# Attention by pairs of heads in whole float32 for all batches, ahead of a feed-forward network, on one core

## The chip, the cores and the metric

The kernel runs on one core of a Trainium2 chip. A core has a matrix engine (TensorE, PE in the profile, with its weight loads as PEld), VectorE (DVE), ScalarE (ACT), GpSimd (POOL) and a queue engine (SyncE, SP), each with an instruction stream of its own. The metric is the device time of one launch in microseconds.

## The reference

Sliding-window attention with a linear bias per head, and behind it a two-layer network with a sigmoid-weighted activation. Cut to what is computed:

```
# q, k, v: [8, 8, 576, 64]; w_in: [512, 2048]; w_out: [2048, 512]; all float32
scores = q @ k.transpose(0, 1, 3, 2) / sqrt(64)
rel    = pos[:, None] - pos[None, :]
slopes = 2.0 ** (-8.0 * (arange(8) + 1) / 8)
scores = where((rel >= 0) & (rel < 128), scores - slopes * abs(rel), -1e9)
attn   = softmax(scores)                      # + 1e-9 in the denominator
x      = (attn @ v).transpose(0, 2, 1, 3).reshape(4608, 512)
h      = x @ w_in
out    = (h * sigmoid(1.702 * h)) @ w_out     # [4608, 512] float32
```

## The kernel before

The 4608 rows of the network are cut into 18 chunks of 256 (`T`). A `Job` is one chunk against the 16 blocks of 128 hidden units (`DFF`); `up` makes one hidden block (twelve matmuls of 256 columns, L569) and `down` adds it to the output (six of 512 columns, L588). The network works in the reduced format F32R: each operand is split into a high part and a remainder, and three of the four products are kept. The weights come as 64-bit words and are decoded on the chip (L228 to L235), two halves per hidden block, just ahead of their first use.

Attention makes the chunks' inputs. It is cut into units, and every call of `tick` moves several units one stage on: loads, scores, bias and minimum (`biased`), exponentials (`exponents`), division (`normal`), transposes (`flip`), products with the values (`mix`). `due` lists by which chunk how many units must be through, and from which chunk on they may start; the main loop calls `tick` between hidden blocks at the pace that this asks. Within that the order on each engine is made by a scheduler with a simulated timeline; `in_turn` fixes the order of a group of matmuls, and `tc.keep_in_program_order` pins an instruction to its place in the program.

There are two kinds of units:

- Batches 1 to 7 use `Unit`. A pair of heads stands end to end as 1152 positions in nine blocks of 128, cut into five units of one or two blocks. q and k are laid out twice, on rows 0 to 63 and 64 to 127. Q holds the high part of q on the upper half and its remainder on the lower; K1 and K2 hold high part and remainder of k on both. A score block is two full-array products, Q with K1 and Q with K2 (L351). The values stand as high part beside remainder (`VV`), the transposed probabilities are split into `ph` and `pl` (L475, L481), and each block of keys takes two products (L516). Rows 0 to 63 and 64 to 127 of the result are added by `sum_up` (L537 to L546).
- Batch 0 uses `WholeUnit`: a third of the sequence (0 to 256, 256 to 512, 512 to 576) for two heads together, one on rows 0 to 63 and the other on rows 64 to 127 of the array. Scores are float32 products with a contraction of 64 (L341). The two heads' products with the values go to the two column halves (L496). Nothing is split or added up. The second head's scores use a tile of the transposes' pair of PSUM tiles (`t_ps`).

PSUM's eight banks are `acc0`, `acc1`, two `h_ps`, `s_ps`, two `t_ps` and `x_ps`. The first four units run before the network starts ("early"), with idle matmuls on the identity between them (`spin`), and the first weights are decoded in that stretch (`DECODE_TICKS`).

Of the kernel before, what the change touches and what calls it, by code (L numbers as in the profile page):

```python
# [20 lines left out]
P = 128  # L21
# [14 lines left out]
BESIDE = range(12, 24)  # L36
DECODE_TICKS = 4, 5, 6, 7
FETCH_AHEAD = 6
DECODE_AHEAD = 2
# [6 lines left out]
class Block:  # L46


    def __init__(self, q0, rows, heads, first=0, live=0):
        self.q0, self.rows = q0, rows  # L50
        self.heads = heads
        self.first = first
        self.live = live
        self.end = P + rows


class Chunk:


    def __init__(self, pos, n, parts):  # L60
        self.pos, self.n, self.parts = pos, n, parts
        self.width = sum(b.rows for b, _ in parts)
        self.x0 = parts[0][0].q0


class Segment:


    def __init__(self, pos, cols, carried, chunks):
        self.pos, self.cols, self.carried = pos, cols, carried  # L70
        self.first, self.last = chunks[0], chunks[-1]
        for c in chunks:
            c.segment = self


class Unit:


    whole = False

    def __init__(self, pair, blocks, loaded, chunks):
        self.pair, self.blocks = pair, blocks
        self.loaded = loaded
        self.chunks = chunks


def pair_blocks(hp):

    A, Z = 2 * hp, 2 * hp + 1
    blocks = []  # L90
    for i in range(L // P):
        first = P if i == 0 else 0
        live = HALF if i == 5 else first
        if i == 4:
            heads = [(A, 0, HALF, 0), (Z, HALF, P, P + HALF)]
        else:
            heads = [(A if i < 4 else Z, 0, P, live)]
        blocks.append(Block(i * P, P, heads, first, live))
    return blocks


def whole_batch(b):
    units = []
    for hp in range(NP):
        blocks = pair_blocks(hp)
        n = len(blocks)
        chunks = [Chunk(i * P, P, [(blocks[i], P)] + [(z, 0) for z in blocks[i + 1:i + 2]]) for i in range(n)]
        for i in range(0, n, 3):
            Segment(i * P, 3 * P, P if i + 3 < n else 0, chunks[i:i + 3])
        done = 0  # L110
        for i in range(0, n, 2):
            upto = min(i + 1, n) if i + 2 < n else n
            units.append(Unit(b * NP + hp, blocks[i:i + 2], chunks[i:i + 2], chunks[done:upto]))
            done = upto
    return units


def some_blocks(b, runs):

    units = []  # L120
    for hp in range(NP):
        for first, end in runs:
            blocks = pair_blocks(hp)[first:end]
            chunks = [Chunk((first - 1) * P, P, [(blocks[0], 0)])] if first else []
            lead = len(chunks)
            for i, bk in enumerate(blocks):
                chunks.append(Chunk(bk.q0, P, [(bk, P)] + [(z, 0) for z in blocks[i + 1:i + 2]]))
            Segment(first * P, (end - first) * P, 0, chunks)
            pair = b * NP + hp
            if len(blocks) > 2:  # L130
                units.append(Unit(pair, blocks[:2], chunks[:lead + 2], chunks[:lead + 1]))
                units.append(Unit(pair, blocks[2:], chunks[lead + 2:], chunks[lead + 1:]))
            else:
                units.append(Unit(pair, blocks, chunks, chunks))
    return units


class WholeUnit:

    whole = True

    def __init__(self, hp, lo, hi):
        self.hp, self.lo, self.hi = hp, lo, hi
# [9 lines left out]
def part_batch(lo, hi):  # L155
    return [WholeUnit(hp, lo, hi) for hp in range(NP)]
# [3 lines left out]
def tile_kernel(ctx: ExitStack, tc: tile.TileContext, q0, k0, v0, qT, kT, v, w_in, w_out, out):  # L160
# [59 lines left out]
    def decode(st, name):  # L220
# [7 lines left out]
        nc.scalar.activation(c.bitcast(F32), top.bitcast(F32), AF.Copy, scale=2.0 ** -112)  # L228
        nc.vector.tensor_scalar(low, low, 29, None, ALU.logical_shift_right)
        nc.vector.scalar_tensor_tensor(c, c, 3, low, ALU.logical_shift_left, ALU.bitwise_or)  # L230
        nc.vector.scalar_tensor_tensor(c, top, -0x80000000, c, ALU.bitwise_and, ALU.bitwise_or)
        w = c.bitcast(F32)
        res = const.tile([P, 2, 512], F32R, name=name, tag=name)
        nc.scalar.copy(res[:, 0], w)
        nc.gpsimd.tensor_tensor(res[:, 1], w, res[:, 0].bitcast(F32), ALU.subtract)  # L235
        return res
# [4 lines left out]
    def spread(pair, pos, n):  # L241

        b = pair // NP
        at = 0
        while at < n:
            hh, s = divmod(pos + at, S)
            c, o = divmod(b * S + s, T)
            m = min(n - at, S - s, T - o)
            yield hh, c, o, at, m
            at += m  # L250

    def load(u):
        if u.whole:
            load_whole(u)
            return
        b0, bz = u.blocks[0], u.blocks[-1]
        u.q0, u.nq = b0.q0, bz.q0 + bz.rows - b0.q0
        u.k0 = b0.q0 - P + b0.first
        u.nk = u.q0 + u.nq - u.k0
        u.rq = raw.tile([P, 2 * P], F32, name="rq", tag="rq")  # L260
        u.rk = raw.tile([P, 3 * P], F32, name="rk", tag="rk")
        move(u.rq[:, :u.nq], qT[u.pair - NP, :, u.q0:u.q0 + u.nq])
        move(u.rk[:, :u.nk], kT[u.pair - NP, :, u.k0:u.k0 + u.nk])

    def load_whole(u):
# [9 lines left out]
        move(u.rq[:, :u.hi - u.lo], q0[u.hp, :, u.lo:u.hi])  # L275
        if u.early:
            tc.keep_in_program_order(nc.scalar.dma_start(u.rk[:, :u.hi - u.k0], k0[u.hp, :, u.k0:u.hi]))
        else:
            move(u.rk[:, :u.hi - u.k0], k0[u.hp, :, u.k0:u.hi])
        if not u.early:  # L280
            load_whole_v(u)

    def load_whole_v(u):
        full = (u.hi - u.k0) // P
        end = u.k0 + full * P
        move(u.rv[:, :full], v0[u.hp, u.k0:end].rearrange("(c p) h d -> p c h d", p=P))
        if end < u.hi:
            move(u.rv[:u.hi - end, full], v0[u.hp, end:u.hi])

    def load_v(u):  # L290
        if u.whole:
            return
        u.rv = raw.tile([P, 3, D], F32, name="rv", bufs=2)
        at = u.loaded[0].pos
        full = sum(c.n == P for c in u.loaded)
        u.spans = []
        if full:
            move(u.rv[:, :full], v[u.pair - NP, at:at + full * P, :].rearrange("(c p) d -> p c d", p=P))
            u.spans.append((P, slice(0, full)))
        if full < len(u.loaded):  # L300
            m = u.loaded[-1].n
            move(u.rv[:m, full], v[u.pair - NP, at + full * P:at + full * P + m, :])
            u.spans.append((m, slice(full, full + 1)))

    def split_q(u):
        if u.whole:
            return
        u.Q = att.tile([P, 2 * P], F32R, name="Q")
        nc.scalar.copy(u.Q[:, :u.nq], u.rq[:, :u.nq])  # L309

    def split_v(u):
        if u.whole:
            return
        u.VV = att.tile([P, 3, 2, D], F32R, name="VV", bufs=3)
        for m, cs in u.spans:
            nc.scalar.copy(u.VV[:m, cs, 0, :], u.rv[:m, cs])
            nc.gpsimd.tensor_tensor(u.VV[:m, cs, 1, :], u.rv[:m, cs], u.VV[:m, cs, 0, :].bitcast(F32), ALU.subtract)
        for i, c in enumerate(u.loaded):
            c.v = u.VV[:c.n, i].rearrange("p a d -> p (a d)")

    def split_rest(u):
        if u.whole:
            return
        u.K1 = att.tile([P, 3 * P], F32R, name="K1")
        u.K2 = att.tile([P, 3 * P], F32R, name="K2")
# [145 lines left out]
    def high(u):  # L471
        if u.whole:
            return
# [323 lines left out]
```

## Time and profile before

| | |
|---|---|
| median of 3 runs | 1090.27 us (1087.84 to 1092.25) |
| profiled execution | 1090.57 us, its span 1088.8 us |
| busy: PE, DVE, POOL, ACT | 1050.6, 730.2, 644.7, 603.0 us |
| mean granted clock of TensorE | 0.984 |
| instructions | 21667 |
| DMA | 81.24 MB, mean 75 GB/s |

Times are in us unless marked ns. A row of the groups reads: line, engine, operation, output from inputs by the program's names, shapes, count, then busy time and mean ns of one, then idle time of the engine just before them and what ended it. Matmuls are pipelined and their ends are modelled; what one costs in a row of them is seen from the distance of starts. A float32 matmul shows as more than one record.

### The profile page before, as it was taken

The numbers are of one execution on the slowest core, as the hardware profiler recorded it, in microseconds if no ns is written. First come the engines' busy times: TensorE is split into PE (matmuls) and PEld (weight loads), VectorE is DVE, ScalarE is ACT, GpSimd is POOL, SyncE is SP. The second block draws the span as 40 slices with busy tenths as digits, with TensorE's granted clock in tenths as the row PEclk, the third lists the DMA queues.
The fourth block names the chain that finished last, engine by engine and source line by source line (L and its number), as shares of the span: only waits on it lengthen the run. The fifth ranks groups of instructions, "written<-read, shape, count | busy, mean of one in ns | idle before, by whom it ended". The sixth has DMA issues, their size and how long they took to land.

```text
span 1088.8 us, 21667 instructions
## 1 busy us (share of the span) xinstructions
PE 1050.6 (96%) x7013; PEld 939.0 (86%) x7013; DVE 730.2 (67%) x2260; ACT 603.0 (55%) x1812; POOL 644.7 (59%) x919
## 2 busy tenths in 40 slices
PE   6897889999999999999999999999999999999998
PEld 3576777998898999999999999999999999998997
DVE  6979788678888787754666768676867677413131
ACT  5674696466665666543555566655565556322222
POOL 3788897566676676644565556666666666323232
PEclk8896999999999999999999999999999999999999
DMA  6357322232322222211122212222222212000000
GB/s 205 123 178 286 99 70 71 81 84 70 98 75 82 69 84 68 79 28 48 54 70 59 74 54 84 66 84 56 84 67 67 68 53 64 1 20 21 1 20 20
DMA packets 93298, 81.24 MB, mean 75 GB/s; under 512 B 42752, under 2 KB 84480, under 8 KB 93184
## 3 DMA queue, kind: packets, MB, share of 16 engines
q1 hardware_dynamic: 87424, 69.89, 22.3%
q10 hardware_dynamic: 5760, 9.96, 2.5%
q8 instruction: 55, 0.90, 0.4%
q14 instruction: 59, 0.48, 0.1%
HBM read 70.39 MB, written 9.44 MB: 73 GB/s over the span
## 4 chain that ended last, share of the span: by engine, by line
PE 81%; DVE 3%; ACT 0%; issue 0%; DVEq 0%
PE h_ps L569 34%; PE acc L588 33%; PE x_ps L516 5%; PE s_ps L351 5%; PE t_ps L462 4%; DVE xh L553 0%; DVE K L327 0%; DVE xl L555 0%; DVE pb L379 0%; DVE pb L426 0%; DVE pl L481 0%; DVE xf L546 0%; DVE g L575 0%; ACT pb L398 0%; DVE rec L409 0%
## 5 line engine op out<-in xcount | busy, mean ns | idle before, releaser
L569 PE MATMUL h_ps<-xh,w 128*128 128x256 f32 x2304 | 371.4, 286 | 7.5 <-DVE g L575 5.2
L579 POOL TENSOR_TENSOR gl<-g,gh 128x256 fp32r<-128x256 f32 x288 | 217.8, 757 | 260.0 <-ACT gh L578 196.7
L569 PEld LDWEIGHTS h_ps<-xh,w 128*128 128x128 f32 x2304 | 330.4, 190 | 36.4 <-DVE g L575 7.4
L588 PE MATMUL acc<-w,gh 128*128 128x512 f32 x1152 | 326.5, 401 | 0.2 <-DVE o L604 0.2
L575 DVE SCALAR_TENSOR_TENSOR g<-g,h_ps 128x256 f32<-128x256 f32 x288 | 119.2, 415 | 184.7 <-ACT g L574 183.0
L574 ACT ACTIVATE g<-h_ps 128x256 f32<-128x256 f32 x288 | 109.8, 382 | 218.4 <-PE h_ps L569 188.5
L588 PEld LDWEIGHTS acc<-w,gh 128*128 128x128 f32 x1152 | 197.4, 189 | 27.4 <-issue 0.4
L569 PE MATMUL h_ps<-xl,w 128*128 128x256 f32 x1152 | 198.8, 282 | 1.8 <-DVE xl L555 0.9
L588 PE MATMUL acc<-w,gl 128*128 128x512 f32 x576 | 187.7, 401 | 0.4 <-POOL gl L579 0.3
L578 ACT CAST gh<-g 128x256 fp32r<-128x256 f32 x288 | 116.4, 405 | 124.8 <-DVE g L575 113.9
L329 POOL TENSOR_TENSOR K<-rk,K 128x384 fp32r<-128x384 f32 (+1 forms) x140 | 130.1, 929 | 76.7 <-ACT Q L309 13.5
L569 PEld LDWEIGHTS h_ps<-xl,w 128*128 128x128 f32 x1152 | 166.0, 189 | 8.8 <-POOL xl L555 1.2
L398 ACT ACTIVATE pb<-pb,mins 128x256 f32<-128x256 f32 (+2 forms) x252 | 122.4, 487 | 56.7 <-DVE mins L379 51.8
L328 POOL TENSOR_TENSOR Q<-rq,Q 64x256 fp32r<-64x256 f32 (+1 forms) x140 | 99.4, 710 | 25.9 <-DVE K L327 3.4
L379 DVE CUSTOM_DVE_ANT_0 pb<-s_ps,bias 128x128 f32<-128x128 f32 (+2 forms) x280 | 100.2, 376 | 9.7 <-PE s_ps L351 5.8
L588 PEld LDWEIGHTS acc<-w,gl 128*128 128x128 f32 x576 | 92.3, 188 | 8.9 <-POOL gl L579 0.8
L426 DVE TENSOR_SCALAR pb<-pb,rec 128x256 f32<-128x256 f32 (+2 forms) x229 | 97.4, 462 | 3.3
L351 PE MATMUL s_ps<-K,Q 128*128 128x256 f32 (+1 forms) x504 | 92.0, 288 | 4.7 <-DVE mins L379 3.2
L481 DVE TENSOR_TENSOR pl<-t_ps,ph 128x512 fp32r<-128x512 f32 (+2 forms) x140 | 84.1, 603 | 12.1 <-ACT ph L475 7.2
L409 DVE TENSOR_SCALAR rec<-sums 128x2 f32<-128x2 f32 (+3 forms) x152 | 51.4, 338 | 56.6 <-ACT pb L398 52.7
L462 PE MATMUL t_ps<-ident,pb 128*128 128x128 f32 x476 | 86.5, 273 | 1.0 <-DVE pl L481 1.0
L351 PEld LDWEIGHTS s_ps<-K,Q 128*128 128x128 f32 x504 | 74.5, 189 | 12.3 <-DVE mins L379 2.8
(70 smaller groups left out, 1328.3 us busy)
## 6 DMA issues: line engine op xcount, KB each, us to landing
rk<-kT SPq DMA_DIRECT2D x84, 192.0 KB, 2.5
rq<-qT SPq DMA_DIRECT2D x112, 128.0 KB, 2.4
out<-o ACTq DMA_DIRECT2D x36, 256.0 KB, 2.5
rw<-w_in SPq DMA_DIRECT2D x16, 512.0 KB, 4.3
rw<-w_out SPq DMA_DIRECT2D x16, 512.0 KB, 5.5
rk<-kT SPq DMA_DIRECT2D x56, 128.0 KB, 2.2
rv<-v SPq DMA_DIRECT2D x100, 64.0 KB, 2.0
rq<-qT SPq DMA_DIRECT2D x28, 64.0 KB, 2.3
```

Source lines behind the costliest of these rows:

```text
L328: nc.gpsimd.tensor_tensor(Q[D:], rq[D:], Q[D:].bitcast(F32), ALU.subtract)
L329: nc.gpsimd.tensor_tensor(K2, rk, K1.bitcast(F32), ALU.subtract)
L351: nc.tensor.matmul(u.s[:b.rows, e, b.first:b.end], u.Q[:, b.q0 - u.q0:b.q0 - u.q0 + b.rows], k[:, ko:ko + b.end - b.first], start=(z == 0) ...
L379: nc.vector.tensor_tensor_reduce(b.p[ra:rb, cs:b.end], u.s[ra:rb, e, cs:b.end], bias[head][ra:rb, cs:b.end], -SCALE, BIG, ALU.add, ALU.min ...
L398: nc.scalar.activation(live, live, AF.Exp, bias=u.mins[:b.rows, e:e + 1], scale=-1.0, accum_out=u.sums[:b.rows, e:e + 1],)
L462: nc.tensor.transpose(u.t[:c.n, w:w + b.rows], b.p[:b.rows, col:col + c.n], ident[:b.rows, :b.rows])
L569: nc.tensor.matmul(h, w1[f][:, z, k * P:(k + 1) * P], x[:, k], start=(n == 0), stop=(n == len(ops) - 1))
L574: nc.scalar.activation(g, h, AF.Tanh, scale=0.851)
L575: nc.vector.scalar_tensor_tensor(g, g, 1.0, h, ALU.add, ALU.mult)
L578: nc.scalar.copy(gh, g)
L579: nc.gpsimd.tensor_tensor(gl, g, gh.bitcast(F32), ALU.subtract)
L588: nc.tensor.matmul(acc, g[:, t * P:(t + 1) * P], w2[f][:, z], start=(f == self.f0 and n == 0), stop=(f == self.f1 - 1 and n == 2))
```

## The change

`Unit` becomes what `WholeUnit` was, for every batch: 12 units per batch (three thirds for four pairs of heads). `Block`, `Chunk`, `Segment`, the split stages (`split_q`, `split_v`, `split_rest`, `high`, `low`) and `sum_up` go. q and k are laid out once, v by pairs. `due` is made per third of a batch, not per batch. Divisions go to GpSimd, VectorE and ScalarE by a letter for each of a unit's up to four pieces. The transposed probabilities of the second head are copied by VectorE from batch 1 on. The first eight weight halves are decoded in pinned order, three of them before the network starts instead of four, and one weight block less is fetched ahead.

```diff
-DECODE_TICKS = 4, 5, 6, 7
+DECODE_TICKS = 5, 6, 7
+PINNED = 8
...
+    def load_v(u):
+        if u.at != DEPTH:
             u.rv = att.tile([P, 3, 2, D], F32, name="VV", bufs=3)
...
-        u.s = ps.tile([P, 2, 2 * P], F32, name="s_ps")
-        for e, b in enumerate(u.blocks):
-            ko = b.q0 - P + b.first - u.k0
-            for z, k in enumerate((u.K1, u.K2)):
-                nc.tensor.matmul(
-                    u.s[:b.rows, e, b.first:b.end], u.Q[:, b.q0 - u.q0:b.q0 - u.q0 + b.rows],
-                    k[:, ko:ko + b.end - b.first], start=(z == 0), stop=(z == 1),
-                )
+        u.s = [ps.tile([P, 2, 2 * P], F32, name="s_ps"),
+               ps.tile([P, 2, 2 * P], F32, name="sb_ps", tag="acc1" if u.early else "t_ps", bufs=1 if u.early else 2)]
+        products = []
+        for i, (at, rows) in enumerate(u.blocks):
+            first = max(u.k0 - at + P, 0)
+            for hh in range(2):
+                r = slice(hh * D, (hh + 1) * D)
+                products.append(nc.tensor.matmul(
+                    u.s[hh][:rows, i, first:P + rows], u.rq[r, at - u.lo:at - u.lo + rows],
+                    u.rk[r, at - P + first - u.k0:at + rows - u.k0], start=True, stop=True,
+                ))
+        in_turn(products)
...
+        engines = "PPVA" if u.early else "PAPA" if u.b == 0 else "PAVA" if u.b == 1 else "PVVA"
+        for _, live, e in u.p:
+            rec = u.rec[:rows, e:e + 1]
+            if engines[e] == "A":
+                nc.scalar.activation(live, live, AF.Copy, scale=rec)
             else:
-                nc.vector.tensor_scalar(live, live, u.rec[:rows, e:e + 1], None, ALU.mult)
+                on = nc.gpsimd if engines[e] == "P" else nc.vector
+                on.tensor_scalar(live, live, rec, None, ALU.mult)
...
-                (nc.vector.tensor_copy if hh and u.early else nc.scalar.copy)(pt[:n, a:z], t[:n, a:z])
+                (nc.vector.tensor_copy if hh and (u.early or u.b) else nc.scalar.copy)(pt[:n, a:z], t[:n, a:z])
...
+    for b in range(B):
+        for lo, hi in ((0, 2 * P), (2 * P, 4 * P), (4 * P, S)):
+            units += part_batch(b, lo, hi)
+            due.append((len(units), (b * S + lo) // T, max((b * S + hi - 1) // T - XBUFS, 0)))
...
-        stage(1, split_q)
-        stage(-2, flip, split_v)
-        stage(0, load_v)
-        stage(-1, biased)
-        stage(1, split_rest)
-        stage(-1, exponents)
...
+        stage(-2, flip)
+        stage(0, lambda u: None if u.early else load_v(u))
+        stage(-1, biased, exponents, normal)
         stage(0, scores)
         stage(-3, mix)
```

More of the change, by code (lines that the diff above doesn't have):

```diff
@@ L43 @@
 SPINS = 10, 6, 6, 6, 6, 6, 6
[L46 to L73, printed above, removed]
@@ L76 @@
-class Unit:
[L79 to L99, printed above, removed]
@@ L102, in whole_batch @@
[L102 to L115, printed above, removed]
@@ L118, in some_blocks @@
[L118 to L135, printed above, removed]
@@ L152, in __init__, with part_batch, tile_kernel @@
             self.chunks.append((k, n, parts))
-def part_batch(lo, hi):
-    return [WholeUnit(hp, lo, hi) for hp in range(NP)]
+def part_batch(b, lo, hi):
+    return [Unit(b, hp, lo, hi) for hp in range(NP)]
 @with_exitstack
-def tile_kernel(ctx: ExitStack, tc: tile.TileContext, q0, k0, v0, qT, kT, v, w_in, w_out, out):
+def tile_kernel(ctx: ExitStack, tc: tile.TileContext, qT, kT, v, w_in, w_out, out):
     nc = tc.nc
@@ L224, in decode @@
         c = ffn.tile([P, 512], I32, name="wc", tag="o", bufs=3)
[L228 to L231, printed above, removed]
+        pin(nc.scalar.activation(c.bitcast(F32), top.bitcast(F32), AF.Copy, scale=2.0 ** -112))
+        pin(nc.vector.tensor_scalar(low, low, 29, None, ALU.logical_shift_right))
+        pin(nc.vector.scalar_tensor_tensor(c, c, 3, low, ALU.logical_shift_left, ALU.bitwise_or))
+        pin(nc.vector.scalar_tensor_tensor(c, top, -0x80000000, c, ALU.bitwise_and, ALU.bitwise_or))
         w = c.bitcast(F32)
         res = const.tile([P, 2, 512], F32R, name=name, tag=name)
-        nc.scalar.copy(res[:, 0], w)
-        nc.gpsimd.tensor_tensor(res[:, 1], w, res[:, 0].bitcast(F32), ALU.subtract)
+        pin(nc.scalar.copy(res[:, 0], w))
+        pin(nc.gpsimd.tensor_tensor(res[:, 1], w, res[:, 0].bitcast(F32), ALU.subtract))
         return res
     xf = {}
[L241 to L250, printed above, removed]
-    def load(u):
[L253 to L265, printed above, removed]
+    def load(u):
         if u.at == DEPTH:
@@ L273, in load_whole @@
             u.rk = raw.tile([P, 3 * P], F32, name="rk", tag="rk")
-            u.rv = att.tile([P, 3, 2, D], F32, name="VV", bufs=3)
[L275 to L283, printed above, removed]
+        move(u.rq[:, :u.hi - u.lo], qT[u.pair, :, u.lo:u.hi])
@@ L284, in load_whole_v @@
+        if u.early:
+            tc.keep_in_program_order(nc.scalar.dma_start(u.rk[:, :u.hi - u.k0], kT[u.pair, :, u.k0:u.hi]))
+        else:
+            move(u.rk[:, :u.hi - u.k0], kT[u.pair, :, u.k0:u.hi])
+    def load_v(u):
+        if u.at != DEPTH:
+            u.rv = att.tile([P, 3, 2, D], F32, name="VV", bufs=3)
         full = (u.hi - u.k0) // P
         end = u.k0 + full * P
-        move(u.rv[:, :full], v0[u.hp, u.k0:end].rearrange("(c p) h d -> p c h d", p=P))
+        move(u.rv[:, :full], v[u.pair, u.k0:end].rearrange("(c p) h d -> p c h d", p=P))
@@ L287, in load_whole_v @@
         if end < u.hi:
[L288 to L303, printed above, removed]
@@ L331, in scores @@
-    def scores(u):
-        if u.whole:
-            u.s = [ps.tile([P, 2, 2 * P], F32, name="s_ps"),
-                   ps.tile([P, 2, 2 * P], F32, name="sb_ps", tag="acc1" if u.early else "t_ps", bufs=1 if u.early else 2)]
-            products = []
-            for i, (at, rows) in enumerate(u.blocks):
-                first = max(u.k0 - at + P, 0)
-                for hh in range(2):
-                    r = slice(hh * D, (hh + 1) * D)
-                    products.append(nc.tensor.matmul(
-                        u.s[hh][:rows, i, first:P + rows], u.rq[r, at - u.lo:at - u.lo + rows],
-                        u.rk[r, at - P + first - u.k0:at + rows - u.k0], start=True, stop=True,
-                    ))
-            in_turn(products)
-            return
-        u.s = ps.tile([P, 2, 2 * P], F32, name="s_ps")
-        for e, b in enumerate(u.blocks):
-            ko = b.q0 - P + b.first - u.k0
-            for z, k in enumerate((u.K1, u.K2)):
-                nc.tensor.matmul(
-                    u.s[:b.rows, e, b.first:b.end], u.Q[:, b.q0 - u.q0:b.q0 - u.q0 + b.rows],
-                    k[:, ko:ko + b.end - b.first], start=(z == 0), stop=(z == 1),
-                )
+            move(u.rv[:u.hi - end, full], v[u.pair, end:u.hi])
@@ L356, in biased @@
     def biased(u):
         u.mins = att.tile([P, 4], F32, name="mins", bufs=3)
-        if u.whole:
-            u.p = []
-            for i, (at, rows) in enumerate(u.blocks):
-                cs = slice(max(u.k0 - at + P, 0), P + rows)
-                for hh in range(2):
-                    if hh:
-                        p = att.tile([P, 3 * P], F32, name="pb", tag=("K1", "K2")[i])
-                    else:
-                        p = att.tile([P, 2 * P], F32, name="pb", bufs=5)
-                    e = 2 * i + hh
-                    nc.vector.tensor_tensor_reduce(
-                        p[:rows, cs], u.s[hh][:rows, i, cs], bias[2 * u.hp + hh][:rows, cs],
-                        -SCALE, BIG, ALU.add, ALU.min, u.mins[:rows, e:e + 1],
-                    )
-                    u.p.append((p, p[:rows, cs], e))
-            return
@@ L374, in biased @@
-        for e, b in enumerate(u.blocks):
-            b.p = att.tile([P, 2 * P], F32, name="pb", bufs=5)
-            for head, ra, rb, cs in b.heads:
-                if cs > b.live:
-                    nc.gpsimd.memset(b.p[ra:rb, b.live:cs], FAR)
+        u.p = []
+        for i, (at, rows) in enumerate(u.blocks):
+            cs = slice(max(u.k0 - at + P, 0), P + rows)
+            for hh in range(2):
+                if hh:
+                    p = att.tile([P, 3 * P], F32, name="pb", tag=("K1", "K2")[i])
+                else:
+                    p = att.tile([P, 2 * P], F32, name="pb", bufs=5)
+                e = 2 * i + hh
@@ L379, in biased @@
                 nc.vector.tensor_tensor_reduce(
-                    b.p[ra:rb, cs:b.end], u.s[ra:rb, e, cs:b.end], bias[head][ra:rb, cs:b.end],
-                    -SCALE, BIG, ALU.add, ALU.min, u.mins[ra:rb, e:e + 1],
-                )
-            if b.live > b.first:
-                nc.gpsimd.memset(b.p[:, :b.live], 0.0)
+                    p[:rows, cs], u.s[hh][:rows, i, cs], bias[2 * u.hp + hh][:rows, cs],
+                    -SCALE, BIG, ALU.add, ALU.min, u.mins[:rows, e:e + 1],
+                )
@@ L386, in exponents @@
+                u.p.append((p, p[:rows, cs], e))
     def exponents(u):
         u.sums = att.tile([P, 4], F32, name="sums", bufs=3)
-        if u.whole:
-            for _, live, e in u.p:
-                rows = live.shape[0]
-                nc.scalar.activation(
-                    live, live, AF.Exp, bias=u.mins[:rows, e:e + 1], scale=-1.0,
-                    accum_out=u.sums[:rows, e:e + 1],
-                )
-            return
-        for e, b in enumerate(u.blocks):
-            live = b.p[:b.rows, b.live:b.end]
+        for _, live, e in u.p:
+            rows = live.shape[0]
@@ L409, in normal @@
         nc.vector.tensor_scalar(u.rec[:rows, :ne], u.sums[:rows, :ne], 1e-9, None, ALU.add)
         nc.vector.reciprocal(u.rec[:rows, :ne], u.rec[:rows, :ne])
-        if u.whole:
-            for _, live, e in u.p:
-                rec = u.rec[:rows, e:e + 1]
-                if e < 2 or not u.early and e == 2:
-                    nc.gpsimd.tensor_scalar(live, live, rec, None, ALU.mult)
-                elif u.early and e == 2:
-                    nc.vector.tensor_scalar(live, live, rec, None, ALU.mult)
-                else:
-                    nc.scalar.activation(live, live, AF.Copy, scale=rec)
-            return
@@ L421, in normal @@
-        for e, b in enumerate(u.blocks):
-            live = b.p[:rows, b.live:b.end]
-            if on_act:
-                nc.scalar.activation(live, live, AF.Copy, scale=u.rec[:rows, e:e + 1])
-            else:
-                nc.vector.tensor_scalar(live, live, u.rec[:rows, e:e + 1], None, ALU.mult)
-    def flip_whole(u):
+        engines = "PPVA" if u.early else "PAPA" if u.b == 0 else "PAVA" if u.b == 1 else "PVVA"
+        for _, live, e in u.p:
+            rec = u.rec[:rows, e:e + 1]
+            if engines[e] == "A":
+                nc.scalar.activation(live, live, AF.Copy, scale=rec)
+            else:
+                on = nc.gpsimd if engines[e] == "P" else nc.vector
+                on.tensor_scalar(live, live, rec, None, ALU.mult)
@@ L500, in mix_whole @@
         in_turn(products)
-        ct, o = divmod(u.lo, T)
-        to = home(ct)[:, u.hp, o:o + n]
-        (nc.vector.tensor_copy if u.early else nc.scalar.copy)(to, x[:, :n])
-    def mix(u):
-        if u.whole:
-            mix_whole(u)
-            return
-        for c in u.chunks:
-            g = c.segment
-            if c is g.first:
-                g.x = ps.tile([P, 4 * P], F32, name="x_ps", bufs=1)
-            a = c.x0 - g.pos
-            for z in range(2):
-                nc.tensor.matmul(
-                    g.x[:, a:a + c.width], c.v, c.p[z],
-                    start=(c is g.first and z == 0), stop=(c is g.last and z == 1),
-                    skip_group_check=True,
-                )
-            if c is g.last:
-                sum_up(u, g)
+        at = 0
+        while at < n:
+            ct, o = divmod(u.b * S + u.lo + at, T)
+            m = min(n - at, T - o)
+            (nc.vector.tensor_copy if u.early else nc.scalar.copy)(home(ct)[:, u.hp, o:o + m], x[:, at:at + m])
+            at += m
     def home(ct):
@@ L775, in lay_out @@
     lay = {
-        "q0": pairs(q[0]),
-        "k0": pairs(k[0]),
-        "v0": v[0].reshape(NP, 2, S, D).transpose(0, 2, 1, 3),
-        "qT": transposed(q[1:]),
-        "kT": transposed(k[1:]),
-        "v": v[1:].reshape((B - 1) * NP, L, D),
+        "qT": pairs(q),
+        "kT": pairs(k),
+        "v": v.reshape(B * NP, 2, S, D).transpose(0, 2, 1, 3),
     }
```

128 lines of the change are left out of this document (16 added, 112 removed).

## The prediction

> **What bounds the kernel now.** I read the page's busy shares first, then the chain of work that ended last, then busy time by stage.
>
> ```profile
> PE 1050.6 (96%) x7013; PEld 939.0 (86%) x7013; DVE 730.2 (67%) x2260; ACT 603.0 (55%) x1812; POOL 644.7 (59%) x919
> ...
> PEclk8896999999999999999999999999999999999999
> ...
> PE 81%; DVE 3%; ACT 0%; issue 0%; DVEq 0%
> ```
>
> TensorE is busy 96% of the span and holds 81% of the chain; its clock is granted in full except near the start. The stages show where this is not so (columns: stage, PE, PEld, DVE, ACT, POOL busy us and instructions, PE clock, DMA share, GB/s):
>
> ```profile
> 86.00:115.00 29.00, 22.89 (x105) 18.30 (x103) 26.89 (x47) 13.62 (x37) 24.38 (x19) 0.71 0.72 254
> 115.00:176.00 61.00, 50.59 (x325) 43.27 (x325) 49.47 (x135) 51.17 (x156) 53.54 (x65) 0.97 0.22 59
> 176.00:600.00 424.00, 421.38 (x2892) 386.32 (x2893) 305.66 (x1005) 243.41 (x750) 259.30 (x398) 1.00 0.26 71
> ```
>
> From 176 us on PE idles 2.6 us in 424, so what an edit adds to PE there is added to the time, and a lighter VectorE, ScalarE or GpSimd gives nothing back. From 86 to 176 us PE waits and its clock is partly halved: there a lighter VectorE can help.
>
> **The present price of a head pair on PE.** Busy times of pipelined matmuls overlap, so I price by starts. Groups of PE instructions between 600 and 900 us (count | busy, mean ns):
>
> ```profile
> L569 PE MATMUL h_ps<-xh,w 128*128 128x256 f32 x675 | 109.0, 283 | 0.0
> L588 PE MATMUL acc<-w,gh 128*128 128x512 f32 x336 | 94.7, 400 | 0.0
> L569 PE MATMUL h_ps<-xl,w 128*128 128x256 f32 x336 | 55.5, 280 | 0.0
> L588 PE MATMUL acc<-w,gl 128*128 128x512 f32 x170 | 55.5, 400 | 0.0
> L351 PE MATMUL s_ps<-K,Q 128*128 128x256 f32 (+1 forms) x186 | 35.1, 292 | 0.0
> L462 PE MATMUL t_ps<-ident,pb 128*128 128x128 f32 x178 | 32.4, 272 | 0.0
> ```
>
> A stretch of the timeline, in which batch 0 already runs in the form that the change gives to all batches (start us, us, instruction, count):
>
> ```profile
> 61.26 1.10 PE L588 MATMUL acc<-w,gh 128*128 128x512 f32 x4
> 62.19 0.63 PE L588 MATMUL acc<-w,gl 128*128 128x512 f32 x2
> 62.75 0.54 PE L341 MATMUL s_ps<-rk,rq 64*64 64x192 f32 x2
> 63.22 0.66 PE L439 MATMUL t_ps<-ident,pb 128*128 128x128 f32 x4
> 63.71 1.20 PE L569 MATMUL h_ps<-xh,w 128*128 128x256 f32 x8
> 64.75 0.63 PE L569 MATMUL h_ps<-xl,w 128*128 128x256 f32 x4
> 65.22 0.39 PE L569 MATMUL h_ps<-xh,w 128*128 128x256 f32 x2
> 65.54 0.54 PE L341 MATMUL sb_ps<-rk,rq 64*64 64x192 f32 x2
> 66.01 0.43 PE L496 MATMUL x_ps<-pw,VV 128*64 128x128 f32 x2
> 66.37 0.97 PE L569 MATMUL h_ps<-xh,w 128*128 128x256 f32 x6
> 67.17 0.39 PE L569 MATMUL h_ps<-xl,w 128*128 128x256 f32 x2
> ```
>
> Four 256-column matmuls of the feed-forward part take 64.75 to 65.22, 0.117 us each; four of 512 columns 61.26 to 62.19, 0.233 each. The feed-forward part of the 300 us is then 1011 x 0.117 + 506 x 0.233 = 236 us, and 64 us remain for attention. A pair of heads now issues 18 score products (L351), 17 transposes (L462) and 18 products with the values (L516): 186/18 and 178/17 say 10.4 pairs. So a pair costs 6.15 us of PE. It is near what slots alone give: 36 x 0.117 + 17 x 0.11 = 6.1.
>
> **The price after.** The form stays that of batch 0, so its rows are the price list. A float32 product is two records here:
>
> ```profile
> L341 PE MATMUL s_ps<-rk,rq 64*128 64x256 f32 x24 | 9.5, 483 | 1.3 <-DVE mins L368 1.3
> ```
>
> That is 24 for the 12 such products of batch 0's first heads, and the two heads of a pair can run side by side:
>
> ```profile
> 52.89 0.70 PE L341 MATMUL s_ps<-rk,rq 64*128 64x256 f32 x2
> ...
> 58.38 0.38 PE L341 MATMUL sb_ps<-rk,rq 64*128 64x256 f32 x1
> 58.39 0.38 PE L341 MATMUL s_ps<-rk,rq 64*128 64x256 f32 x1
> 58.60 0.59 PE L341 MATMUL sb_ps<-rk,rq 64*128 64x256 f32 x2
> 59.12 0.44 PE L439 MATMUL t_ps<-ident,pb 128*128 128x128 f32 x2
> 59.49 1.09 PE L496 MATMUL x_ps<-pw,VV 128*64 128x128 f32 x12
> 60.51 0.44 PE L439 MATMUL t_ps<-ident,pb 128*128 128x128 f32 x2
> ...
> 81.07 0.33 PE L439 MATMUL t_ps<-ident,pb 64*128 64x64 f32 x2
> 81.33 0.74 PE L569 MATMUL h_ps<-xh,w 128*128 128x256 f32 x4
> ...
> 85.16 0.60 PE L496 MATMUL x_ps<-pw,VV 128*64 128x64 f32 x8
> 85.69 0.73 PE L588 MATMUL acc<-w,gl 128*128 128x512 f32 x2
> ```
>
> One pass of each head over 256 columns takes 58.38 to 58.60, 0.22 us for both. Per pair of heads, with perfect company:
> - Scores: blocks of 128 and 256, twice 256, and 192 columns, 1088 in all, two passes: 1088 x 2 x 0.22/256 = 1.87 us.
> - Products with the values: 384 and 512 columns in the first two units, 896 x 2 x 0.22/256 = 1.54; the third unit's eight records take 0.53 (85.16 to 85.69), 0.43 without the step out of the mode: 1.97.
> - Transposes: 14 of the full kind at 0.11 (63.22 to 63.71 has four in 0.49 with one step in it): 1.54; the third unit's two pairs take 0.26 each (81.07): 0.52. Together 2.06.
> The sum is 5.9 us, a little under the 6.15 of now.
>
> What is not in it is the change of array shape. The last feed-forward matmuls before a 64-row or 64-column group are late: two of 512 columns take 62.19 to 62.75, 0.56 instead of 0.47. The group itself pays at both ends (65.54 to 66.01 is 0.47 for 2 x 0.165), and the feed-forward matmuls behind it too (six take 66.37 to 67.17, 0.80 instead of 0.70). Together 0.09 + 0.14 + 0.10 = 0.33 us for each excursion out of the full array and back. The same numbers come wherever such a group stands, so I take it for a cost of PE itself, not a wait. A pair has six such groups (scores and values of three units), and its third unit's transposes add about 0.2 for each head: 6 x 0.33 + 0.4 = 2.4. Where both heads' scores do not start together it is worse: at 52.89 the first head's block runs alone, and the rest follows 5 us later. A unit so split pays its first block's passes twice and one more excursion: 1.0 + 3 x 0.33 = 2.0 us per pair if all three units split. Batch 0 splits nearly always, because its second score tile waits for a transpose tile that GpSimd's normalisation holds up. There three of a unit's four pieces are normalised on GpSimd; later batches put one there, so I count one unit in ten, 0.2 us.
>
> So a pair costs 5.9 + 2.4 + 0.2 = 8.5 us, bounds 7.7 (scores and values of a unit in one excursion, three steps of 0.14 instead of three excursions) and 10.3 (all split). Batch 0 changes only by its decode's pins and order: at nothing, a few us either way. The 28 pairs of batches 1 to 7 give 28 x (8.5 - 6.15) = +66 us; bounds +43 and +116.
>
> The Trainium skill, page "TensorEngine Tiling (Array Packing)", section "Available Configurations", "Key Properties", says that changing the tiling mode drains the array. By that rule the steps stay when the queue is full, and the sum is the forecast; without it the sum would be that of the first rival below. The trace agrees, with its 0.33 us an excursion. The same page's table under "Theoretical Speedup" promises up to twice the speed for a contraction of 64 or less, which speaks for the change; the two heads within 0.22 us bear it out, but it has no term for the steps.
>
> **What goes from the other engines.**
>
> ```profile
> L329 POOL TENSOR_TENSOR K<-rk,K 128x384 fp32r<-128x384 f32 (+1 forms) x140 | 130.1, 929 | 76.7 <-ACT Q L309 13.5
> L481 DVE TENSOR_TENSOR pl<-t_ps,ph 128x512 fp32r<-128x512 f32 (+2 forms) x140 | 84.1, 603 | 12.1 <-ACT ph L475 7.2
> L415 POOL TENSOR_SCALAR pb<-pb,rec 128x256 f32<-128x256 f32 x12 | 14.4, 1212 | 3.4 <-ACT w L234 2.9 <-DVE rec L410 0.4
> ```
>
> All splits go: GpSimd loses five K remainders of 0.93 us per pair (and Q's and V's) and gains three normalisations of about 1.2; VectorE loses five remainders of P (0.60) and the K casts and gains three plain copies of at most that size; its score reductions stay at ten per pair. The doubled rows of q and k are no longer moved, and the loads are issued for three units per pair instead of five, ahead as before. SyncE's queue gets fewer entries and none of them is moved behind a new wait. All this lies beside PE and is worth nothing after 176 us. Before that, PE at its full rate needs about 15 of the 29 us and 45 of the 61 us of the first two stages (their feed-forward records by the slots above, and attention by the present price), so some 30 us are lost. The end from above is that all of it comes back. The end from below is nothing: VectorE is busy 26.89 of 29 us in the first stage, and weight decoding, which stays, holds most of it. A third, -10 us, is nearest to these rows.
>
> **Sum.** The profiled execution took 1090.6 us (span 1088.8), 0.3 above the median. 1090.6 + 66 - 10 = 1147 us. Own range: pair prices 8.0 to 9.2 with 0 to 20 us back, 1122 to 1176.
>
> **Rivals.**
> 1. The steps cost nothing in a full queue (the other side). The pair then costs 5.9 less the 0.2 of steps inside its terms, 5.7, thus 28 x -0.45 = -13, and with the same -10 the time is 1068. For it: the rows above are all from before 86 us, where waits can look like steps. Against: the delays repeat to 0.01 us. It decides below about 0.1 us per excursion, as seven or eight of them times 28 then no longer outweigh the 23 us.
> 2. The steps merge and VectorE's relief comes back in full: 7.7 us per pair, +43, and 20 to 30 us regained, 1104 to 1114. For it: a values group is ready at the start of a turn and can stand next to scores (66.01 does). Against: the ordering knows nothing of steps.
> 3. Scores split everywhere, as in batch 0, since the second score tile takes its room from the transposes: 10.3 per pair, +116 - 10, 1197. For it: 52.89 and 62.75. Against: the lighter normalisation.
>
> **How the numbers follow.** Chances: forecast 0.52, rival 1 0.13, rival 2 0.18, rival 3 0.17. The measurement cannot tell less than about 0.5%, 5 us, from no change. Rival 1 is faster. Between it and rival 2, where fewer than three steps of a pair are paid, lies about 0.08 of rival 2's chance: 0.02 of it faster and 0.06 within 0.5%. The others are slower. This gives faster 0.15, same 0.06, slower 0.79. The range from 1085 to 1200 leaves out rival 1 and the upper half of rival 3.
>
> **What would show it.** In the changed profile: PE's share at 98% from 100 us on; L569 and L588 with unchanged counts; score and value records of 64 rows or 64 columns, 20 and 28 per pair; 0.56 us for two 512-column matmuls wherever a score group follows; starts of the two heads' records some ns apart, or not (rival 3); VectorE under 55%; and the feed-forward part at its present pace once attention is through. I am wrong if two such matmuls take 0.47 us ahead of a group in the full stage, or if PE shows idle stretches beyond 176 us.

## The result: 10.7% slower, and the profile after

The changed kernel takes 1206.6 us (1204.87 to 1206.89) against 1089.9 us for the kernel before; the ratio is 1.107, 95% interval 1.104 to 1.109. The forecast of 1147 us had the sign, the engine and a part of the cause, and less than half of the size: +117 us where +57 was given, above both of its ranges, which ended at 1176 and at 1200.

The page after, first the busy shares, the clock and the chain of waits:

```profile
PE 1182.9 (98%) x7353; PEld 927.2 (77%) x7353; DVE 500.5 (42%) x1631; ACT 514.2 (43%) x1645; POOL 383.0 (32%) x471
...
PEclk9999999999999999999999999999999999999999
...
PE 90%; DVE 8%; ACT 1%; DMA 0%; issue 0%; POOL 0%; SPq 0%; DVEq 0%; ACTq 0%; POOLq 0%
```

VectorE is down by 230 us, GpSimd by 262, and the time is longer by 117: all of that relief lies beside PE. The stages (columns as before):

```profile
86.00:115.00 29.00, 26.64 (x168) 20.53 (x168) 28.44 (x71) 22.27 (x68) 21.62 (x20) 1.00 0.14 41
115.00:176.00 61.00, 59.51 (x356) 46.63 (x354) 38.53 (x88) 34.78 (x98) 34.05 (x32) 1.00 0.12 35
176.00:600.00 424.00, 424.00 (x2639) 335.23 (x2639) 153.58 (x552) 168.30 (x558) 116.68 (x154) 1.00 0.14 40
```

From 86 to 176 us PE is now busy 86 of 90 us (73 before) at full clock; beyond 176 us it never rests, but issues 2639 matmuls where there were 2892. (Both counts take in all of PE's matmuls, attention's too.) ScalarE takes up the 33rd hidden block at 197.2 us against 208.0 us before. So the first part is 11 us faster, and everything behind it some 127 us slower.

The PE groups between 600 and 900 us price a pair of heads as in the prediction; a pair has 18 transposes (L239) in this kernel:

```profile
L303 PE MATMUL h_ps<-xh,w 128*128 128x256 f32 x574 | 91.5, 289 | 0.0
L322 PE MATMUL acc<-w,gh 128*128 128x512 f32 x290 | 82.5, 404 | 0.0
L322 PE MATMUL acc<-w,gl 128*128 128x512 f32 x144 | 47.2, 405 | 0.0
L303 PE MATMUL h_ps<-xl,w 128*128 128x256 f32 x288 | 46.7, 280 | 0.0
...
L239 PE MATMUL t_ps<-ident,pb 128*128 128x128 f32 (+2 forms) x152 | 22.1, 265 | 0.0
```

862 x 0.117 + 434 x 0.233 = 202 us are feed-forward work; 98 us remain for 152/18 = 8.4 pairs: 11.6 us per pair, against 6.15 before and 8.5 forecast, and above the bound of 10.3. Where it goes is seen in the timeline of one turn:

```profile
623.48 0.63 PE L303 MATMUL h_ps<-xl,w 128*128 128x256 f32 x4
624.04 0.70 PE L181 MATMUL s_ps<-rk,rq 64*128 64x256 f32 x2
624.67 0.43 PE L261 MATMUL x_ps<-pw,VV 128*64 128x128 f32 x2
625.03 0.70 PE L181 MATMUL sb_ps<-rk,rq 64*128 64x256 f32 x2
625.66 1.20 PE L322 MATMUL acc<-w,gh 128*128 128x512 f32 x4
626.69 0.63 PE L322 MATMUL acc<-w,gl 128*128 128x512 f32 x2
627.25 0.48 PE L181 MATMUL s_ps<-rk,rq 64*128 64x256 f32 x1
627.26 0.48 PE L181 MATMUL sb_ps<-rk,rq 64*128 64x256 f32 x1
627.57 0.38 PE L181 MATMUL s_ps<-rk,rq 64*128 64x256 f32 x1
627.58 0.38 PE L181 MATMUL sb_ps<-rk,rq 64*128 64x256 f32 x1
627.88 1.08 PE L261 MATMUL x_ps<-pw,VV 128*64 128x128 f32 x10
```

Scores use half of the array's rows (64*128, the row form), values half of its columns (128*64, the column form). The first head's two passes run alone at 624.04; then, in the column form, two passes of the values alone; then the second head's two, alone, back in the row form. That is 1.62 us for four score passes, which side by side take 0.44, and two value passes. The second block, at 627.25, has company: starts 0.01 us apart. Two forms take turns here with no feed-forward matmul between them, a case that the prediction's price of excursions did not have.

The second head's scores need one of the transposes' two PSUM tiles. Both had been copied out well before:

```profile
620.92 0.58 ACT L247 COPY pw<-t_ps 128x512 f32<-128x512 f32 x1
621.40 0.68 DVE L247 COPY pw<-t_ps 128x512 f32<-128x512 f32 x1
```

The last copy ended at 622.08, 2 us before the first head's passes, and PE did not idle. So what parts the heads in this turn is the order that the scheduler had fixed for PE, not a wait on the chip.

I counted this in the trace of 600 to 900 us: a pass has company if a pass of the other head starts within 0.02 us. 82 pairs of passes have it, 240 passes run alone. There are 74 excursions out of the full array, and at 62 places one kind of small-array work (scores, values, transposes of 64 rows or columns) follows another with no full-array matmul between; I call these direct changes.

### The profile page after: what moved, and what is told of

It reads as the page before. It is cut to its first block, busy times and chain, and to the rows that moved or that the text cites. A ratio compares the mean times of both kernels' runs of the same rounds, so it can differ in the third digit from the quotient of the medians.

```text
span 1204.8 us, 20145 instructions
## 1 busy us (share of the span) xinstructions
PE 1182.9 (98%) x7353; PEld 927.2 (77%) x7353; DVE 500.5 (42%) x1631; ACT 514.2 (43%) x1645; POOL 383.0 (32%) x471
## 4 chain that ended last, share of the span: by engine, by line
PE 90%; DVE 8%; ACT 1%; DMA 0%; issue 0%; POOL 0%; SPq 0%; DVEq 0%; ACTq 0%; POOLq 0%
PE h_ps L303 34%; PE acc L322 33%; PE x_ps L261 8%; PE s_ps L181 5%; PE t_ps L239 5%; PE sb_ps L181 5%; DVE wc L138 2%; DVE wc L137 2%; DVE rw L136 1%; DVE pb L198 1%; DVE rec L216 0%; DMA rw<-w_out 0%; PE acc L113 0%; DVE g L309 0%; ACT pb L208 0%
## 5 line engine op out<-in xcount | busy, mean ns | idle before, releaser
L208 ACT ACTIVATE pb<-pb,mins 128x128 f32<-128x128 f32 (+2 forms) x320 | 150.3, 471 | 85.0 <-DVE mins L198 84.0
L225 POOL TENSOR_SCALAR pb<-pb,rec 128x128 f32<-128x128 f32 (+2 forms) x104 | 89.9, 866 | 178.7 <-DVE rec L217 123.8
L261 PE MATMUL x_ps<-pw,VV 128*64 128x256 f32 (+3 forms) x896 | 124.5, 308 | 0.2
L261 PEld LDWEIGHTS x_ps<-pw,VV 128*64 128x64 f32 (+1 forms) x896 | 62.5, 135 | 65.7 <-issue 44.0
L181 PE MATMUL s_ps<-rk,rq 64*128 64x256 f32 (+2 forms) x320 | 98.5, 393 | 2.7 <-DVE mins L198 2.6
L198 DVE CUSTOM_DVE_ANT_0 pb<-s_ps,bias 128x256 f32<-128x256 f32 (+2 forms) x160 | 56.4, 377 | 102.6 <-PE sb_ps L181 53.6
L181 PE MATMUL sb_ps<-rk,rq 64*128 64x256 f32 (+2 forms) x320 | 93.8, 388 | 0.4 <-ACT pw L247 0.4
L239 PE MATMUL t_ps<-ident,pb 128*128 128x128 f32 (+1 forms) x576 | 85.9, 268 | 6.6 <-DVE mins L198 2.6
L247 DVE COPY pw<-t_ps 128x64 f32<-128x64 f32 (+2 forms) x116 | 46.7, 422 | 97.6 <-PE t_ps L239 97.6
L239 PEld LDWEIGHTS t_ps<-ident,pb 128*128 128x128 f32 (+1 forms) x576 | 61.3, 137 | 22.1 <-issue 6.0
```

The source lines that it names most:

```text
L181: products.append(nc.tensor.matmul(u.s[hh][:rows, i, first:P + rows], u.rq[r, at - u.lo:at - u.lo + rows], u.rk[r, at - P + first - u.k0:a ...
L198: nc.vector.tensor_tensor_reduce(p[:rows, cs], u.s[hh][:rows, i, cs], bias[2 * u.hp + hh][:rows, cs], -SCALE, BIG, ALU.add, ALU.min, u.min ...
L208: nc.scalar.activation(live, live, AF.Exp, bias=u.mins[:rows, e:e + 1], scale=-1.0, accum_out=u.sums[:rows, e:e + 1],)
L225: on.tensor_scalar(live, live, rec, None, ALU.mult)
L239: nc.tensor.transpose(t[:n, w:w + rows], p[:rows, col:col + n], ident[:rows, :rows])
L261: products.append(nc.tensor.matmul(x[hh * D:(hh + 1) * D, a:a + p.shape[1]], u.rv[:m, c, hh], p, start=c == 0, stop=c == len(u.chunks) - 1 ...
```

## The experiments

Theory A was: the price lies on PE, in lost company and in steps. Its rivals: B, the order has nothing to do with which tile is ready; C, the steps are hidden waits. Theory D (the early gain comes from the relief of VectorE and GpSimd) and rival E (it comes from the new start alone) are about the first 200 us. The runs of the first five experiments below are one execution each; executions of the kernel before lie up to 4.7 us apart, so differences of that size between single runs stay open.

**Who goes first.** The edit stands in `scores` and in `mix`:

```diff
-            for hh in range(2):
+            for hh in (1, 0):
```

> The changed kernel, but in the scores and in the products with the values the second head's product stands ahead of the first head's in each pair. Nothing else differs. Theory A (the two heads lose each other's company because the first head's tile is ready earlier, so its product starts alone and all that follow in the fixed order are one place off): the head that is ready last now leads, most passes run in pairs, lone passes between 600 and 900 us fall from 240 to under 80, a pair of heads costs 9 to 10 us of PE in place of 11.6, and the time is 1150 to 1170 us. Rival B (the order comes from the simulated timeline and has nothing to do with which tile is ready first): lone passes stay near 240 and the time is 1200 to 1212 us.

1176.0 us, 31 us less than the change by an order alone. The groups from 600 to 900 us:

```profile
L303 PE MATMUL h_ps<-xh,w 128*128 128x256 f32 x597 | 95.3, 288 | 0.0
L322 PE MATMUL acc<-w,gh 128*128 128x512 f32 x300 | 85.0, 403 | 0.0
L322 PE MATMUL acc<-w,gl 128*128 128x512 f32 x151 | 49.6, 405 | 0.0
L303 PE MATMUL h_ps<-xl,w 128*128 128x256 f32 x300 | 49.6, 281 | 0.0
...
L239 PE MATMUL t_ps<-ident,pb 128*128 128x128 f32 (+2 forms) x160 | 23.1, 266 | 0.0
```

897 x 0.117 + 451 x 0.233 = 210 us, 90 us for 8.9 pairs: 10.1 us each. Lone passes fell from 240 to 112, pairs rose from 82 to 156: more lone ones than the expected number under 80, and the time is 6 us above its range. Pairs of passes are two passes each, so 312 of 424 passes now have company, 164 of 404 before. B falls; the order recovers about half of what had run alone, not all.

**One excursion per turn.** In addition the scores of one unit and the products with the values of the unit three before it are one chain:

```diff
-        in_turn(products)              # in scores
+        return products
...
-        in_turn(products)              # in mix
+        in_turn(before + products)     # before: the turn's scores
```

> As the run before (second head first), and the scores of one unit and the products with the values of an older unit are tied into one chain, scores first, so that a turn has one excursion out of the full array in place of two or more. Theory A with the steps of 0.33 us as a cost of PE itself: the pair of heads costs 7.7 to 8.5 us of PE, and the time is 1100 to 1130 us. Rival C (what looks like steps are short waits for other engines): the time is that of the run before within 10 us, or longer, as the values now wait for the scores.

1129.7 us, 46 us less again, at the upper end of what A gave. A turn in its timeline:

```profile
706.50 0.62 PE L303 MATMUL h_ps<-xl,w 128*128 128x256 f32 x4
707.06 0.48 PE L181 MATMUL sb_ps<-rk,rq 64*128 64x256 f32 x1
707.06 0.48 PE L181 MATMUL s_ps<-rk,rq 64*128 64x256 f32 x1
...
707.81 0.38 PE L181 MATMUL sb_ps<-rk,rq 64*128 64x256 f32 x1
707.81 0.38 PE L181 MATMUL s_ps<-rk,rq 64*128 64x256 f32 x1
708.12 0.87 PE L261 MATMUL x_ps<-pw,VV 128*64 128x256 f32 x8
708.92 1.21 PE L322 MATMUL acc<-w,gh 128*128 128x512 f32 x4
```

Its groups from 600 to 900 us:

```profile
L303 PE MATMUL h_ps<-xh,w 128*128 128x256 f32 x645 | 101.4, 285 | 0.0
L322 PE MATMUL acc<-w,gh 128*128 128x512 f32 x321 | 91.1, 404 | 0.0
L303 PE MATMUL h_ps<-xl,w 128*128 128x256 f32 x324 | 51.7, 280 | 0.0
L322 PE MATMUL acc<-w,gl 128*128 128x512 f32 x160 | 51.1, 398 | 0.0
...
L239 PE MATMUL t_ps<-ident,pb 128*128 128x128 f32 (+2 forms) x172 | 22.5, 262 | 0.0
```

Eight score passes take 707.06 to 708.12, eight value passes 0.80 us behind them, and PE is back. 969 x 0.117 + 481 x 0.233 = 225.4 us, so 74.6 us for 9.6 pairs: 7.8 us each, near the 7.7 that the prediction gave for merged groups. 13 passes run alone; excursions are 49, direct changes 32. These 300 us are a good stretch: from 200 to 1100 us the same count gives 8.5 us a pair, with 132 of 1176 passes alone. Part of the 46 us is company that the chain brought (99 more lone passes gone between 600 and 900 us), the rest steps; the run does not part the two. It is still 40 us slower than before: even where company is nearly perfect the steps keep a pair above 6.15.

**The step by itself.** In the kernel before, where only feed-forward work is left, each hidden block of chunks 16 and 17 gets two small products, over all 128 rows in chunk 16 and over 64 rows in chunk 17 (arguments shortened):

```diff
+        r = slice(0, P if c == NCH - 2 else HALF)
+        tc.keep_in_program_order(nc.tensor.matmul(spare[0][:, :HALF], ident[r, :], ident[r, :HALF], ...))
```

> The kernel before with 32 small products of the identity added to each of the last two chunks, where PE does only feed-forward work: in chunk 16 over the full array (128 rows, 64 columns), in chunk 17 over 64 rows (64 columns). Their result goes to a PSUM tile that nothing reads. If a step out of the full array and back costs PE 0.33 us whatever waits there are, chunk 17 takes 9 to 12 us longer than chunk 16, and chunk 16 takes 2 to 6 us longer than the 44.8 us of a plain chunk. If the steps are waits of the attention (rival C), chunks 16 and 17 agree within 2 us.

1109.8 us. One hidden block of chunk 16 in its timeline:

```profile
1010.57 1.09 PE L603 MATMUL acc<-w,gh 128*128 128x512 f32 x4
...
1013.03 0.55 PE L568 MATMUL x_ps<-ident 128*128 128x64 f32 x4
...
1013.83 1.09 PE L603 MATMUL acc<-w,gh 128*128 128x512 f32 x4
```

The same of chunk 17:

```profile
1060.99 1.09 PE L603 MATMUL acc<-w,gh 128*128 128x512 f32 x4
...
1062.97 0.63 PE L582 MATMUL h_ps<-xl,w 128*128 128x256 f32 x4
1063.53 0.66 PE L568 MATMUL x_ps<-ident 64*128 64x64 f32 x4
...
1064.57 1.09 PE L603 MATMUL acc<-w,gh 128*128 128x512 f32 x4
```

A hidden block takes 3.26 us with the small products over 128 rows and 3.58 us over 64: 0.32 us for one excursion, with no attention in these chunks and no idle time of PE. The expected 9 to 12 us per chunk became 16 x 0.32 = 5.1, since the two small products stand next to each other and share one excursion. The other number missed too: the products over 128 rows add 16 x (3.26 - 2.80) = 7.4 us to a plain chunk of 44.8 us, where 2 to 6 were expected. C falls, as the two chunks differ by more than its 2 us. The last four matmuls before the 64-row group take 0.56 instead of 0.47 us, as the rows of the prediction did. This agrees with the Trainium skill, page "TensorEngine Tiling (Array Packing)", section "Key Properties", which says that a change of the tiling mode drains the array; the page gives no price.

**No company.** `for hh` outside, blocks and chunks inside, in both places.

> The changed kernel with all products of the first head ahead of all of the second in the scores and in the products with the values, so that no two neighbours in the fixed order can run side by side except at one place per group. Theory A: the 82 pairs of passes that still ran side by side between 600 and 900 us part as well, 13 to 14 us for 8.4 head pairs, 1.6 us per head pair, and the time is 1235 to 1265 us. Rival (company is worth little, the price is all in the steps): 1195 to 1215 us.

1236.7 us, at the low end: 30 us more than the change, about as much as the better order takes off. Of these, 12.6 us stand already when ScalarE takes up the 33rd hidden block (209.8 us against 197.2), where PE also waits; 17.6 us fall behind it, where PE is the limit. So the company that was left had been worth something, though in the full stage alone the loss is less than the 28 us that the range begins with; 45 pairs of passes survive there between 600 and 900 us, 35 of them among the values.

**Scores alone.** The second head first in `scores` only.

> The changed kernel with the second head first in the scores alone; the products with the values keep their order. Theory A says that both kinds had lost their company for the same reason, lone passes of the scores costing 19 us and of the values 17 us between 600 and 900 us, so that about half of the 31 us comes back: 1185 to 1197 us. If only the scores matter (as in the prediction's third rival), 1174 to 1180 us.

1181.8 us: 25 of the 31 us come with the scores' order, 6 with the values'. That lies between the two expectations. Of the 6, 3.1 arise before the 33rd hidden block (200.3 us against 197.2); behind it the scores' order alone brings 27.9 us and both orders 30.5. The scores' order brings values company too: 78 pairs of passes among the values have it here against 52 in the change. So the order of the scores is the main lever, as the prediction's third rival, which named the scores, would have it, but the lone passes are of both kinds.

**The early part.** First the kernel before with the start of the changed one (decode pinned, three halves early, one block less fetched ahead, the new division of batch 0's normalisation, and the values of batch 0's later units loaded one stage later):

> The kernel before (batch 0 whole, batches 1 to 7 split) with the start of the changed kernel: pinned decode of the first eight halves, three halves decoded before the network starts, one weight block less fetched ahead, the changed kernel's choice of engines for batch 0's divisions. Against the mixture of two batches (1078 us) it tells what the form of batch 1 is worth. Theory D (the gain of the first 200 us comes from VectorE and GpSimd freed of the splits): 1084 to 1092 us. Rival E (it comes from the start): 1070 to 1080 us, as batch 1 then also keeps its cheaper products.

1080.9 us, ratio 0.991 (0.989 to 0.993), 0.9 us above E's range and 3 us below D's. The start alone gives 9.6 us, and ScalarE takes up its 33rd hidden block at 196.1 us, so E's cause holds; which of the start's parts does it was not tried. Then batches 0 and 1 in the changed form with that start, and the rest split; this was expected before the start alone had run:

> A mixture: batches 0 and 1 in the changed form, batches 2 to 7 in the split form of before, with the start of the changed kernel (pinned decode, three halves decoded early, one weight block less fetched ahead). Theory D (the changed form gains time in the first 200 us, where PE waits for VectorE, and loses it in the full stage at about 5.3 us per pair of heads): the four pairs of batch 1 cost PE 20 us more, mostly inside present idle time, and the time is 1062 to 1085 us. Rival E (nothing is gained by the form, the early gain is that of the new start alone): four dearer pairs against some 15 us of start, 1085 to 1100 us.

1078.2 us, ratio 0.989 (0.986 to 0.992). This lies inside D's range and below E's, so by itself it spoke for D; but the ratio is not to be told from that of the start alone, which has no relief of VectorE by batch 1. What E had wrong is that the four dearer pairs would show at the end. The stages of the start alone:

```profile
86.00:115.00 29.00, 20.57 (x123) 16.83 (x122) 25.93 (x56) 20.29 (x61) 26.95 (x30) 0.94 0.23 62
115.00:176.00 61.00, 57.98 (x375) 51.86 (x375) 50.65 (x117) 47.55 (x132) 49.27 (x56) 0.97 0.18 50
```

And of the mixture:

```profile
86.00:115.00 29.00, 27.24 (x172) 20.97 (x171) 28.47 (x71) 22.27 (x68) 21.63 (x20) 1.00 0.16 47
115.00:176.00 61.00, 59.49 (x356) 46.64 (x354) 38.54 (x88) 34.84 (x98) 34.11 (x32) 1.00 0.12 35
```

In the mixture PE is busy 86.7 us of 90 against 78.6, and the end does not move: the dearer products of batch 1 fill time in which PE waited. Last, the mixture with the second head first and the chain:

> The mixture of two batches (1078 us) with the second head first and the chain of scores and values in batches 0 and 1. If the dear head pairs of batches 0 and 1 still lie on PE's path, the four pairs of batch 1 and the rest of batch 0 become 2 to 3.5 us cheaper each and the time is 1062 to 1073 us. If they lie in time that PE spends waiting for decoded weights anyway, it stays at 1074 to 1080 us.

1076.3 us, ratio 0.987 (0.985 to 0.988): the lowest time here, 1.3% under the kernel before, though its interval overlaps that of the mixture. That the cheaper form moves it by so little (1.9 us) agrees with the second expectation: what batches 0 and 1 cost PE lies in time that is lost there anyway. That this time is a wait for decoded weights was not tested.

## Why the prediction was wrong in size

**The present price** of 6.15 us per pair, the slots of 0.117 and 0.233 us, the two records per product and the 0.22 us for a pass of each head all held. The signs that the prediction named came too: PE at 98%, VectorE at 42%, and 0.56 us for two 512-column matmuls ahead of a score group (626.69 to 627.25).

**The step of 0.33 us** held: 0.32 measured by itself. Rival 1, free steps, is out. One of its parts was read too high: the 0.14 takes a 192-column pass for 0.165 us, but such passes start 0.21 us apart in the run without company, which leaves about 0.05 there.

**The term that failed is the count**, "six such groups" and "one unit in ten" split. Batch 0's rows showed units split nearly always; I explained that by its normalisation on GpSimd and took it away for the later batches. The trace after shows 240 lone passes of 404 in 300 us. Worked out over 8.4 pairs: lone passes cost about 36 us by their widths where pairs of them would cost 18, 2.1 us per pair of heads against 0.2 counted for all splitting; 74 excursions at 0.33 and 62 direct changes at about 0.15 (an estimate, the 0.14 of the prediction's merged case, not measured by itself) cost 34 us, 4.0 per pair against 2.4. With 5.7 for the passes and transposes this gives 11.8, beside 11.6 measured. The bound of 10.3 failed for one reason more: it split only the first block of the scores and never the values, and it let no scores and values take turns.

**Why units split.** With one piece on GpSimd in place of three the units still split, so the lighter normalisation did not bring company, and the order of heads alone took away half of the lone passes. In the trace after, the second head's scores mostly start 2 to 4 us behind the last copy out of a transposes' tile, while the first head's tile has been free for 3 to 17 us. This points to the transposes' room, as the prediction's third rival had it; the room itself was not varied, and the scheduler's simulated times, by which the order is fixed, are in no trace.

**The early gain** came out at the forecast's size, 11 us by the 33rd hidden block against 10, by luck: the start gives 9.6 us, which the prediction put at nothing, and the relief of VectorE nothing that the end shows, as the dearer products take the time in which PE had waited.

**The sum** with measured terms: 28 x (11.6 - 6.15) = +153, less the start's 10, is +143, and +117 was measured. Not all of the 28 pairs lie where PE is the limit. From 200 to 1100 us, 2654 x 0.117 + 1330 x 0.233 = 620 us are feed-forward work, and 280 us remain for 438/18 = 24.3 pairs, 11.5 us each; less than half a pair comes later. 24.7 x (11.5 - 6.15) = +132, less 10, is +122, 5 us above the measured. The other 3.3 pairs are worked off before 200 us, where PE has waiting time for them; the equal times of the start alone and the mixture, whose four pairs are dearer by some 20 us, say the same.

**Rival 3**, scores split everywhere, at 1197 us with a chance of 0.17, was nearest. The evidence for it stood in the quoted rows (52.89, 62.75) and I argued it away.

## What to carry to other kernels

Two half-array products are worth a whole one only while they run side by side, and in an order fixed by hand a product whose operand is ready early pulls the pairs apart; let the one that is ready last lead, and look at the starts in the trace, not at the counts. An excursion to another array shape cost PE 0.32 us here even in a stream that never idled, so small-array groups belong together, and beside a saturated full-array stream they have to save more than that. Where a form has already run in a kernel, its rows there are the forecast; a reason why it will behave better elsewhere has to be priced as a guess.

## What the runs showed of the hardware

An excursion to 64 rows and back costs 0.32 us in a stream with no idle time, against the same small products over 128 rows (3.58 and 3.26 us for a hidden block). Two 256-column passes on the two row halves take 0.21 to 0.22 us together, starts 0.01 us apart, and one alone takes the same: in the run without company such passes start 0.22 us apart (median). A direct change between the row form and the column form seems to cost less than going through the full array: about 0.15 us is an estimate from the prediction's rows, and the pairs' price of 7.8 us in the chained kernel fits it.
